# Attention and two expert layers on one core: where 1/sum is spread, how the V products are cut, and the order of two kinds of loads

## The chip, the cores and the metric

The kernel runs on one core of a Trainium2 chip. The metric is the device time of one launch in microseconds (us). The kernel before took 536.39 us, the median of three runs (535.16, 536.39, 536.76).

## What is computed

Attention over 2 batches and 8 heads (576 tokens, 64 dimensions a head) with rotated queries and keys; then two expert layers over the 1152 tokens, both in fp32:

```python
scores = scale * np.matmul(q_rot, k_rot.transpose(0, 1, 3, 2))
attn = np.exp(scores - np.max(scores, axis=-1, keepdims=True))
attn = attn / (np.sum(attn, axis=-1, keepdims=True) + 1e-09)
x = np.matmul(attn, v)                  # to (1152, 512)
h = np.maximum(x @ w_in, 0.0)           # w_in 512x2048
x = h * h @ w_out                       # w_out 2048x512
out = (x @ w_a) * (x @ w_b) @ w2_out    # w_a, w_b 512x1536, w2_out 1536x512
```

## The kernel before

**Who sets the order.** Every piece of work is an operation of a planner (`Plan`, lines 75 to 250). It names the engine or engines that may do it (`FLEX` is VectorE or GpSimd), a cost, the operations that it follows, and the buffers that it takes (`acq`) and gives back (`rel`). TensorE's operations keep the order in which the program writes them; for the other engines the planner plays the program through with its costs and takes, on each engine, the ready operation that is due first. `soon` (with `anchor`) makes an operation due a fixed time after another one, `urgent` lets an engine wait a little for it, and `pl.far` lets work that is due much later stand back. The kernel's engines then run these orders strictly, each waiting at semaphores.

**Attention.** The 16 heads go in 8 pairs (0 to 7). A pair has five score steps (`scores`, line 394): steps 0 to 3 are four TensorE matmuls for 128 queries of both heads (L415), step 4 is a shorter tail (L411). The scores land in one of two wide PSUM slots (`STAGS`, two because `NS` is 2). VectorE copies them out negated with the row minimum (L443, one for each head), ScalarE takes the exponential and the row sum (L448), VectorE transposes 32x32 blocks (L465). The main loop (lines 1080 to 1097) writes, for each step, the scores of the next step, the loads, the V products of the pair before, and the transpose.

**V products.** `times_v` (L501) multiplies 18 blocks of 32 keys, eight small matmuls each, into four PSUM banks (`AV`, columns 0 to 191 of each, accumulated over all 18 blocks). `PARTS` cuts the blocks into five parts, 4, 4, 4, 3 and 3; part c of pair p-1 stands behind the scores that follow step c of pair p. After the last part ScalarE copies the banks out (`xf`, eight copies, L318). The last pair's parts stand between the first pieces of expert layer 1 (`VFILL` says behind which).

**1/sum.** `recip` (L529) makes 1/sum and cuts it in three bf16 pieces. `flip` (L546) transposes these into rows; `spread` (L556) multiplies the rows by a selector, nine small matmuls (L564), so that 1/sum stands in 128 partitions over all queries; ScalarE copies that out in two halves (`inv`, L568); GpSimd multiplies it with `xf` (L587) and splits the result into high and low parts. In step 4 of pair p stand the flip of pair p-1 and the spread of pair p-2, both in one slot of `STAGS` (named r).

**Loads.** In each of steps 0 to 3 `load_part` issues one quarter of the pair's V (L481) and one plane of the keys and queries of pair p+2 (L341). One tiny ScalarE copy into the V buffer's first column (L479), behind the step's last exponential, releases both: SyncE's transfers then wait for that copy. GpSimd rotates the keys and queries (L367).

**Expert layers.** Products in fp32 are three matmuls of high and low halves (L719 to L721). Sixteen and twelve tiles of hidden columns are handled, most of them by a seven-product scheme (`product`, `super1`, `super2`). `split_y` (L839) makes the seven combinations of layer 1's result for layer 2: VectorE or GpSimd subtract (L610, tiles gT), ScalarE casts the high half (L613), VectorE or GpSimd subtract again for the low half. In `super2` the first products are moved out of PSUM by ScalarE (`p1`, `p7`, `p6`: L920, L925, L930) and added or multiplied by VectorE (`p2` L935, `p4` L940, `p5` L946); `p4` needs the bank that L925 empties, `p3` the one that L946 empties.

## Time and profile before

| | |
|---|---|
| median of three runs | 536.39 us |
| profiled execution | 535.2 us, of which the span of the trace is 533.4 us |
| granted TensorE clock | 0.999 of full speed |
| TensorE matmuls busy | 524.1 us (98%) |
| TensorE weight loads busy | 473.1 us (89%), beside the matmuls |
| VectorE busy | 421.1 us (79%) |
| ScalarE busy | 305.1 us (57%) |
| GpSimd busy | 397.4 us (74%) |
| attention, steady part | about 22 to 118 us |

Shares are means over stages with different limits. A timeline row gives the start of an instruction (or of several merged ones, with their count), its length, its engine and line, what it writes and reads, and in brackets the idle time before it with what ended it. Matmul lengths overlap by some 0.1 us, so the spacing of two starts, not the length, is what a piece of TensorE work takes.

### The profile page before, as it was taken

The page shows a single profiled execution, that of the slowest core. Times are in us where ns is not written, and L with a number is a line of the kernel's source. Part 1 is how long each engine was busy: PE and PEld are TensorE (multiplying, and loading weights), DVE is VectorE, ACT ScalarE, POOL GpSimd, SP SyncE. Part 2 cuts the span into 40 slices and gives each one's busy share as a digit, 9 for nine tenths or more (in the row PEclk, how much of TensorE's full clock was granted, in tenths as well). Part 3 has the DMA queues.
Part 4 walks back from the last instruction along what each step waited for, and adds up shares of the span by engine and source line. Part 5 has one row for each costly group of instructions (what it writes and reads, how often), then busy time and mean ns, then how long its engine had stood idle before and what let it go on. Part 6 is the DMA issues. An engine that isn't in the chain of part 4 may idle for free.

```text
span 533.4 us, 13367 instructions
## 1 busy us (share of the span) xinstructions
PE 524.1 (98%) x5390; PEld 473.1 (89%) x5390; DVE 421.1 (79%) x768; ACT 305.1 (57%) x756; POOL 397.4 (74%) x338
## 2 busy tenths in 40 slices
PE   8999999999999999999999998999999999999997
PEld 6666666668999999999999998999999999999996
DVE  5999997996996798678868999767878777878454
ACT  1767886897776784287348544766534444353210
POOL 2866889876998966776868799998888987776110
PEclk9999999999999999999999999999999999999999
...
GB/s 232 212 186 181 181 181 181 149 152 123 119 63 96 120 119 80 119 79 65 106 108 119 53 29 78 80 120 119 80 120 118 80 80 119 119 41 0 1 1 177
DMA packets 18913, 58.48 MB, mean 110 GB/s; under 512 B 2313, under 2 KB 4489, under 8 KB 17828
## 3 DMA queue, kind: packets, MB, share of 16 engines
...
q14 instruction: 19, 0.16, 0.1%
...
## 4 chain that ended last, share of the span: by engine, by line
PE 91%; POOL 3%; DVE 2%; issue 1%; DMA 1%; ACT 0%; SPq 0%; DVEq 0%
PE m L719 13%; PE m L721 13%; PE m L720 13%; PE av L501 9%; PE s L415 8%; PE av L721 6%; PE av L719 6%; PE av L720 6%; PE m L1037 3%; PE m L1038 3%; PE m L1039 3%; PE s L411 2%; PE av L1037 1%; PE av L1038 1%; PE av L1039 1%
## 5 line engine op out<-in xcount | busy, mean ns | idle before, releaser
L610 POOL TENSOR_TENSOR g<-v,g 128x576 fp32r<-128x576 f32 (+1 forms) x26 | 32.0, 1230 | 34.1 <-ACT g L736 34.1
L448 ACT ACTIVATE PV<-PV,st 128x576 f32<-128x576 f32 x48 | 36.9, 769 | 21.7 <-DVE PV L443 20.8
L367 POOL TENSOR_TENSOR X<-X,cs_rot 128x1152 f32<-128x1152 f32 x14 | 36.9, 2636 | 15.2 <-DMA X<-in_qk 13.9
L443 DVE TENSOR_SCALAR_CACHE_REDUCE PV<-s 128x576 f32<-128x576 f32 x48 | 34.5, 746 | 8.9 <-PE s L415 8.8
L772 DVE TENSOR_TENSOR oacc<-m,oacc 128x512 f32<-128x512 f32 (+1 forms) x31 | 21.0, 679 | 14.7 <-PE m L1039 14.6
L721 PE MATMUL m<-g,w_o 128*128 128x384 f32 (+1 forms) x99 | 31.9, 323 | 0.0
L720 PE MATMUL m<-g,w_o 128*128 128x384 f32 (+1 forms) x99 | 31.9, 322 | 0.0
L719 PE MATMUL m<-g,w_o 128*128 128x384 f32 (+1 forms) x99 | 31.9, 322 | 0.0
L920 ACT COPY v<-m 128x288 f32<-128x288 f32 x20 | 8.0, 398 | 39.2 <-PE m L721 39.2
L635 POOL TENSOR_SCALAR cl_i<-cl_i 128x512 f32<-128x512 f32 x14 | 27.2, 1949 | 2.1 <-ACT cl_i L626 2.1
L736 ACT CAST g<-v 128x576 fp32r<-128x576 f32 (+1 forms) x36 | 21.4, 595 | 10.5 <-DVE v L950 9.9
L720 PE MATMUL m<-x,w_pp 128*128 128x288 f32 x92 | 27.2, 295 | 0.0
L721 PE MATMUL m<-x,w_pp 128*128 128x288 f32 x92 | 27.2, 295 | 0.0
L719 PE MATMUL m<-x,w_pp 128*128 128x288 f32 x92 | 27.1, 294 | 0.0
L501 PE MATMUL av<-PT_wb,PV 32*64 32x160 f32 (+1 forms) x1152 | 25.5, 294 | 1.2 <-issue 1.2
L501 PEld LDWEIGHTS av<-PT_wb,PV 32*64 32x64 f32 x1152 | 19.6, 130 | 7.5 <-issue 6.1
L415 PE MATMUL s<-cs_rot 64*128 64x288 f32 x128 | 24.6, 434 | 1.6 <-DVE cs_rot L379 0.8
L415 PE MATMUL s<-rot 64*128 64x288 f32 x128 | 24.8, 433 | 0.7 <-DVE bits_i L632 0.7
L719 PE MATMUL m<-x,w_b 128*128 128x288 f32 x82 | 24.3, 296 | 0.9 <-DVE v L946 0.9
L501 PE MATMUL av<-PT_acc,PV 32*64 32x160 f32 (+1 forms) x1152 | 25.2, 294 | 0.0
L501 PEld LDWEIGHTS av<-PT_acc,PV 32*64 32x64 f32 x1152 | 19.8, 130 | 5.4 <-issue 4.1
L1037 PE MATMUL m<-w_b,g 128*128 128x512 f32 (+1 forms) x63 | 24.6, 390 | 0.0
...
## 6 DMA issues: line engine op xcount, KB each, us to landing
...
```

What stands on the lines that cost most here:

```text
L367: m = pl.op(where, ("s", 2 * S), lambda e, qi=qi: e.tensor_tensor(out=x()[:, :, qi, :], in0=x()[:, :, qi, :], in1=cs, op=ALU.mult), [done[ ...
L415: pe.matmul(s[h]()[:, bk, 0:288], q0, k0[h][:, bk * 288:bk * 288 + 288], start=True, stop=True)
L443: m = pl.op("DVE", ("us", 0.7), lambda e, h=h, j=j: e.tensor_scalar(out=PP[pr.k][:, h, :].rearrange("p (b n) -> p b n", b=2), in0=s[h]()[: ...
L448: x = pl.op("ACT", ("us", 0.8), lambda e, h=h, j=j: e.activation(PP[pr.k][:, h, :], PP[pr.k][:, h, :], AF.Exp, bias=st()[:, 0, j:j + 1], s ...
L501: pe.matmul(AV[a]()[half(h), q], v[r, h, b], pt[r, k:k + 4 + both, 32 * b:32 * b + 32], start=(b == 0), stop=(b == KB - 1), skip_group_che ...
L610: e.tensor_tensor(out=out_, in0=a, in1=b, op=ALU.subtract)
L635: e.tensor_scalar(out=dst(), in0=cl(), scalar1=-HI * TURN, scalar2=HI, op0=ALU.max, op1=ALU.min)
L719: pe.matmul(dst, wh, mh, start=first, stop=False, skip_group_check=open_)
L720: pe.matmul(dst, wh, ml, start=False, stop=False, skip_group_check=open_)
L721: pe.matmul(dst, wl, mh, start=False, stop=last, skip_group_check=open_)
L736: h = pl.op("ACT", ("p" if banked else "s", width), lambda e: e.copy(g()[:, 0, c], v()[:, 0:width]), after + first, acq=acq)
L1037: pe.matmul(b(), gt[:, 0, c], w[:, 0, d], start=(k == 0), stop=False)
```

## The change

Four things. (1) The spread of pair p-2 leaves step 4 of pair p and stands behind the scores of step 1 of pair p; it writes columns 192 to 479 of the first two banks of the V products, of which the products use columns 0 to 191, and the slot r now holds the flip alone. (2) The V products' parts are 2, 4, 4, 5 and 3 blocks. Of the last pair, 10, 5 and 3 blocks instead of 8, 4 and 6 stand behind the first pieces of layer 1. (3) Planes of keys and queries go ahead of the V quarters: two planes after step 0, one V quarter and a plane after step 1, two quarters after step 2, a quarter and a plane after step 3; each transfer has a ScalarE copy of its own that releases it, eight a pair instead of four (four in the last two pairs, which have no keys to load). (4) The y split of the second half is marked `pl.far`.

```diff
--- before.py
+++ after.py
@@ -31,21 +31,21 @@
 NPR = 5
 NS = 2
 KB = 18
-PARTS = ((0, 4), (4, 8), (8, 12), (12, 15), (15, 18))
+PARTS = ((0, 2), (2, 6), (6, 10), (10, 15), (15, 18))
+RUNS = tuple(k for k, (lo, hi) in enumerate(PARTS) if hi > lo)
 NG = 5
 NV = 3
 HB = 288
 PIECES = {"k0": (0, 288), "q0": (0, 192), "k1": (288, 576), "q1": (192, 320), "q2": (320, 576)}
 FIRST = (("k0", "cs"), ("k0", 1), ("q0", 0), ("k1", "cs"), ("k1", 1), ("q1", 0), ("q2", 0))
-VAT = ((0,), (1,), (2,), (3,), ())
-XAT = VAT
+LOADS = ((('x', 0), ('x', 1)), (('v', 0), ('x', 2)), (('v', 1), ('v', 2)), (('v', 3), ('x', 3)), ())
 FAR = 1.5
 WARM = (16, 2, 5, 3)
 EARLY, MID = 1, 4
 GATES = ((0,4),(6,1),(6,3))
 PACE = (27, 5)
 FILL = (-1,1,2,3)
-VFILL = (0,0,1,2,2)
+VFILL = (0,0,0,1,2)
 SOON = 6.0
 LATE = 3.0
 HASTE = 10.0
@@ -302,7 +302,7 @@
     MTAGS = tuple(BANKS)
     WTAGS = ("wa",) + tuple(f"wb{k}" for k in range(NWB))
     pl = Plan({
-        "raw": 3, "bits": 2, "sums": 1, "cl": 2, "wa": NWA, **{f"P{k}": 1 for k in range(NPR)}, **{f"v{k}": 1 for k in range(NV)}, "u": 2, "inv": 1,
+        "raw": 3, "bits": 2, "sums": 1, "cl": 2, "wa": NWA, **{f"P{k}": 1 for k in range(NPR)}, **{f"v{k}": 1 for k in range(NV)}, "u": 2, "inv": 1, "side": 1,
         **{t: 1 for t in STAGS + ("av",)}, **{t: 0 for t in TTAGS + MTAGS + WTAGS[1:]},
         "g0": 1, "g1": 1, "g2": 0, "g3": 0, "g4": 0,
     }, 6.0)
@@ -338,7 +338,7 @@
         if p:
             if p > 1:
                 for k, (qi, n) in enumerate(PLANES):
-                    LX[p, k] = lambda after, k=k, qi=qi, n=n: dma(288, lambda e: e.dma_start(out=b()[:, n, qi], in_=qk[p][:, n, qi]), after, acq=[] if k else [b])
+                    LX[p, k] = lambda after, k=k, qi=qi, n=n: dma(288, lambda e: e.dma_start(out=b()[:, n, qi], in_=qk[p][:, n, qi]), after)
                 return {}
             d = [dma(576, lambda e, qi=qi: e.dma_start(out=b()[:, :, qi], in_=qk[p][:, :, qi]), acq=[b] if qi else []) for qi in (1, 0)]
             return {(qi, n): d[1 - qi] for qi in range(2) for n in range(2)}
@@ -398,6 +398,9 @@
             ST[p] = lazy(lambda: st_p.tile([P, 2, 9], F32, tag="st", name=f"st{p}"))
         r = ROPE[p]
         tail = c == 4
+        side = []
+        if p > 1 and c == 1:
+            side.append(Buf("side", None))
         s = [Buf(STAGS, {t: (lambda t=t, h=h: sps.tile([P, 2, 512], F32, tag=t, name=f"s{p}_{c}_{h}")) for t in STAGS}) for h in range(1 if tail else 2)]
         pr = Buf(f"P{len(EXP) % NPR}", None)
         pr.k = len(EXP) % NPR
@@ -450,12 +453,11 @@
                 bias=st()[:, 0, j:j + 1], scale=-1.0, accum_out=st()[:, 1, j:j + 1]), [m])
             ex.append(x)
         EXP[p, c] = (pr, ex)
-        if tail and p:
+        if p > 1 and c == 1:
+            pl.op(None, None, None, spread(p - 2, side, [lambda h=h: AV[h]()[:, 192:480].rearrange("p (b n) -> p b n", b=2) for h in range(2)]), rel=side)
+        if p and tail:
             x = Buf(STAGS, {t: (lambda t=t: sps.tile([P, 2, 512], F32, tag=t, name=f"r{p}")) for t in STAGS})
-            ends = [flip(p - 1, [x], lambda: x()[:, 1].bitcast(BF16)[0:27, 896:1024])]
-            if p > 1:
-                ends += spread(p - 2, [], [lambda h=h: x()[:, h, 0:288].rearrange("p (b n) -> p b n", b=2) for h in range(2)])
-            pl.op(None, None, None, ends, rel=[x])
+            pl.op(None, None, None, [flip(p - 1, [x], lambda: x()[:, 1].bitcast(BF16)[0:27, 896:1024])], rel=[x])
 
     LV, zeros, fixed = {}, [], []
 
@@ -473,20 +475,28 @@
         more = p + 2 < NPAIR
         if c == 0 and more:
             load_qk_done[p + 2] = load_qk(p + 2)
-        w = ex[-1]
-        for a in VAT[c]:
-            r = slice(32 * a, 32 * a + 32)
-            w = pl.op("ACT", ("us", 0.2), lambda e, r=r: e.copy(V4[r, p % 2, 0, 0, 0:1], st()[r, 1, 2 * c + 1:2 * c + 2]), ex[-1:] + ([AVD[p - 2]] if p > 1 else []))
-            w.soon, w.anchor = 1.8, SDONE[p, c]
-            d = dma(288, lambda e, r=r: e.dma_start(out=V4[r, p % 2], in_=vq[p]), [w])
+        for i, (what, k) in enumerate(LOADS[c]):
+            i = min(i, len(ex) - 1)
+            j = 2 * c + i
+            if what == "x":
+                if not more:
+                    continue
+                qi, n = PLANES[k]
+                x = XA[p + 2]
+                w = pl.op("ACT", ("us", 0.2), lambda e, qi=qi, n=n, j=j: e.copy(x()[0:32, n, qi, 0:1], st()[0:32, 1, j:j + 1]), ex[i:i + 1], acq=[] if k else [x])
+                d = load_qk_done[p + 2][PLANES[k]] = LX[p + 2, k]([w])
+            else:
+                r = slice(32 * k, 32 * k + 32)
+                w = pl.op("ACT", ("us", 0.2), lambda e, r=r, j=j: e.copy(V4[r, p % 2, 0, 0, 0:1], st()[r, 1, j:j + 1]), ex[i:i + 1] + ([AVD[p - 2]] if p > 1 else []))
+                d = dma(288, lambda e, r=r: e.dma_start(out=V4[r, p % 2], in_=vq[p]), [w])
+                LV.setdefault(p, []).append(d)
+            w.soon, w.anchor = 1.0 + 0.7 * i, SDONE[p, c]
             d.late = FAR
-            LV.setdefault(p, []).append(d)
-        for k in XAT[c] if more else ():
-            d = load_qk_done[p + 2][PLANES[k]] = LX[p + 2, k]([w])
-            d.late = FAR
 
     def times_v(p, part):
-        if part == 0:
+        if part not in RUNS:
+            return
+        if part == RUNS[0]:
             AVB[p] = Buf("av", None)
         pt, v = PT[p % 2], V4[:, p % 2]
 
@@ -501,8 +511,8 @@
                         pe.matmul(AV[a]()[half(h), q], v[r, h, b], pt[r, k:k + 4 + both, 32 * b:32 * b + 32], start=(b == 0), stop=(b == KB - 1), skip_group_check=True)
 
         n = PARTS[part][1] - PARTS[part][0]
-        o = pl.op("PE", ("us", 0.05 + 0.255 * n), mm, TOK[p] + LV[p], acq=[] if part else [AVB[p]])
-        if part < len(PARTS) - 1:
+        o = pl.op("PE", ("us", 0.05 + 0.255 * n), mm, TOK[p] + LV[p], acq=[AVB[p]] if part == RUNS[0] else [])
+        if part < RUNS[-1]:
             return
         AVD[p] = o
         xf = XF[p] = vtile(f"xf{p}")
@@ -837,6 +847,11 @@
         pl.op(None, None, None, [t1, t2, t3, t4] + [o for i in range(3, 7) for o in XPART[t][i]], rel=[x])
 
     def split_y(t, b):
+        pl.far = t == 1
+        parts_y(t, b)
+        pl.far = False
+
+    def parts_y(t, b):
         if b == 0:
             YPART[t] = {}
 
```

**TensorE, the tail of a pair and the start of the next.** Before, L411 is the tail's scores, L549 the flip, L564 the spread into slot r, L501 the V products (av are their banks):

```order
L411 MATMUL s_4_0_1367<-rot 64x288 x4
L549 LDWEIGHTS part_1221
L549 MATMUL r_1376<-small,part_1221 27x128
...
L564 MATMUL r_1376<-rows_1135,small 128x128
...
L564 MATMUL r_1376<-rows_1135,small 128x64
L501 MATMUL av_242<-PT_wb,PV 64x160
```

After, L418 is the scores of step 1, L574 the spread, now into the banks av_248 and av_251, L511 the V products of the pair before:

```order
L418 MATMUL s_1_0_1491<-cs_rot 128x288
L418 MATMUL s_1_1_1496<-cs_rot 128x288
...
L574 MATMUL av_248<-rows_1446,small 128x128
...
L574 MATMUL av_251<-rows_1446,small 128x96
...
L574 MATMUL av_251<-rows_1446,small 128x64
L511 MATMUL av_248<-PT_acc,PV 64x160
```

The nine matmuls of the spread moved from the end of one pair to behind step 1 of the next, in front of the first V part there.

**ScalarE, from a pair's second step to its third.** Before, L448 is the exponential, L479 the release of a V quarter and a plane:

```order
L448 ACTIVATE PV,st_1178<-PV,st_1178 128x576
L479 COPY PV<-st_1178 32x1
L448 ACTIVATE PV,st_1178<-PV,st_1178 128x576 x2
L479 COPY PV<-st_1178 32x1
L448 ACTIVATE PV,st_1178<-PV,st_1178 128x576 x2
L479 COPY PV<-st_1178 32x1
L613 CAST x<-x_0_725 128x288
L448 ACTIVATE small,st_1178<-small,st_1178 128x576 x2
```

After, L451 is the exponential, L486 the release of a plane of keys and queries (X), L490 that of a V quarter, L578 the copy of 1/sum out of the V products' bank:

```order
L451 ACTIVATE PV,st_1204<-PV,st_1204 128x576
L486 COPY X_1286<-st_1204 32x1 x2
L451 ACTIVATE PV,st_1204<-PV,st_1204 128x576 x2
L578 COPY inv_1333<-av_248 128x288
L490 COPY PV<-st_1204 32x1
L578 COPY inv_1333<-av_251 128x288
L486 COPY X_1286<-st_1204 32x1
L451 ACTIVATE PV,st_1204<-PV,st_1204 128x576 x2
L490 COPY PV<-st_1204 32x1 x2
```

The two copies of 1/sum stand here now, between the exponentials of steps 1 and 2, with four releases around them where two stood.

**ScalarE at the y split.** Before, L920, L925 and L930 move products of layer 2 out of PSUM, and L613 casts pieces of the split (yacc is layer 1's result):

```order
L613 CAST x<-yacc 128x2x288
L920 COPY v_0_0_4396<-m_1988 128x288
L613 CAST x<-yacc 128x2x288
L925 COPY v_0_0_4396<-m_1977 128x288
L930 COPY u_0_4415<-m_1988 128x288
L613 CAST x<-gT_4387 128x2x288
```

After, L935, L940 and L945 are the moves, L623 the casts, L636 a step of a weight's conversion:

```order
L623 CAST x<-yacc 128x2x288
L636 ACTIVATE cl_4407<-raw_4270 128x512
L935 COPY v_0_0_4416<-av_251 128x288
L940 COPY v_0_0_4416<-av_248 128x288
L623 CAST x<-yacc 128x2x288
L945 COPY u_0_4440<-av_251 128x288
```

The second move out of PSUM now stands in front of the second pair of casts of yacc, not behind it.

**VectorE at the y split.** Before, L610 subtracts pieces of the split (gT), L935, L946 and L940 add from PSUM, L629 is a step of a weight's conversion:

```order
L629 TENSOR_SCALAR av_92<-cl_b_4323 128x512
L610 TENSOR_TENSOR gT_4387<-yacc,gT_4387 128x576
L935 TENSOR_TENSOR v_0_0_4396<-av_242,v_0_0_4396 128x288
L610 TENSOR_TENSOR gT_4387<-yacc,gT_4387 128x576
L946 TENSOR_TENSOR v_0_0_4396<-m_1988,v_0_0_4396 128x288
L940 TENSOR_TENSOR u_0_4415<-m_1977,u_0_4415 128x288
```

After, L620 subtracts, L950, L955 and L961 add from PSUM, L706 adds two pieces of a weight:

```order
L620 TENSOR_TENSOR gT_4405<-yacc,gT_4405 128x576
L950 TENSOR_TENSOR v_0_0_4416<-m_2015,v_0_0_4416 128x288
L706 TENSOR_TENSOR sums_p_4428<-sums_p_4428 128x256
L955 TENSOR_TENSOR u_0_4440<-av_248,u_0_4440 128x288
L961 TENSOR_TENSOR v_0_0_4416<-av_251,v_0_0_4416 128x288
L620 TENSOR_TENSOR parts<-gT_4405,parts 128x576
```

One of the two subtractions of gT in front of the last add from PSUM is gone from VectorE (GpSimd has it), and the add of weight pieces and the third product's add stand there.

## Rows read from the trace of the kernel before

**Rows 1.** Busy time by stage (windows view); first column the stretch in us, then each engine.

```profile
22.00:118.00 96.00, 94.10 (x2278) 64.17 (x2284) 87.47 (x175) 75.33 (x240) 74.69 (x76) 1.00 0.70 178
...
133.00:318.00 185.00, 185.00 (x1237) 184.09 (x1224) 150.98 (x280) 116.91 (x271) 148.22 (x117) 1.00 0.28 92
```

**Rows 2.** TensorE timeline of one pair (start, length, line, operation); a trailing bracket is idle time.

```profile
48.89 1.24 PE L415 MATMUL s<-rot 64*128 64x288 f32 x8
...
51.09 1.97 PE L415 MATMUL s<-rot 64*128 64x288 f32 x8
52.99 1.42 PE L501 MATMUL av<-PT_wb,PV 32*64 32x160 f32 x64
54.34 1.24 PE L415 MATMUL s<-rot 64*128 64x288 f32 x8
55.51 1.37 PE L501 MATMUL av<-PT_wb,PV 32*64 32x160 f32 x64
56.80 1.54 PE L415 MATMUL s<-rot 64*128 64x288 f32 x8
...
60.85 0.49 PE L564 MATMUL r<-rows,small 27*128 27x128 bf16 x9
61.27 1.09 PE L501 MATMUL av<-PT_wb,PV 32*64 32x160 f32 x48
62.29 1.25 PE L415 MATMUL s<-cs_rot 64*128 64x288 f32 x8
```

**Rows 3.** TensorE timeline, V products of pair 5; the bracket is idle time and its releaser.

```profile
90.52 0.49 PE L501 MATMUL av<-PT_wb,PV 32*64 32x128 f32 x4 [1.23 <-issue]
```

**Rows 4.** Waits between 22 and 118 us: total, times, longest.

```profile
POOL X L367 <- DMA X<-in_qk: 13.9, 6, 4.9
```

**Rows 5.** ScalarE timeline of the same pair.

```profile
55.68 0.19 ACT L479 COPY PV<-st 32x1 f32<-32x1 f32 x1
...
56.41 0.78 ACT L448 ACTIVATE PV<-PV,st 128x576 f32<-128x576 f32 x1
...
57.18 0.76 ACT L448 ACTIVATE PV<-PV,st 128x576 f32<-128x576 f32 x1
...
61.41 0.40 ACT L568 COPY inv<-r 128x288 f32<-128x288 f32 x1
```

**Rows 6.** VectorE timeline of the same pair.

```profile
55.61 0.76 DVE L443 TENSOR_SCALAR_CACHE_REDUCE PV<-s 128x576 f32<-128x576 f32 x1 [0.25 <-PE s L415]
...
59.59 1.38 DVE L465 STREAM_TRANSPOSE PT_acc<-PV 128x1152 f32<-128x1152 f32 x1
```

**Rows 7.** TensorE timeline near 324 and 328 us, where the y split stands.

```profile
323.92 0.40 PE L719 MATMUL m<-parts,w_b 128*128 128x288 f32 x1 [0.76 <-ACT v L925]
...
328.30 0.40 PE L719 MATMUL m<-x,w_b 128*128 128x288 f32 x1 [0.95 <-DVE v L946]
```

**Rows 8.** ScalarE timeline there.

```profile
322.89 0.67 ACT L613 CAST x<-yacc 128x576 fp32r<-128x576 f32 x1 [1.64 <-DVE yacc L772]
323.47 0.39 ACT L925 COPY v<-m 128x288 f32<-128x288 f32 x1
```

**Rows 9.** VectorE timeline there, and the same operation earlier.

```profile
304.57 0.76 DVE L610 TENSOR_TENSOR gT<-yacc 128x576 f32<-128x576 f32 x1
...
324.00 1.97 DVE L610 TENSOR_TENSOR gT<-yacc,gT 128x576 f32<-128x576 f32 x1 [0.54 <-POOL gT L610]
...
326.26 1.62 DVE L610 TENSOR_TENSOR gT<-yacc,gT 128x576 f32<-128x576 f32 x1
327.81 0.44 DVE L946 TENSOR_TENSOR v<-m,v 128x288 f32<-128x288 f32 x1
```

**Rows 10.** GpSimd timeline there.

```profile
322.56 2.79 POOL L610 TENSOR_TENSOR gT<-yacc 128x576 f32<-128x576 f32 x2
...
327.23 5.24 POOL L610 TENSOR_TENSOR parts<-gT,parts 128x576 fp32r<-128x576 f32 x3
```

## Prediction, written before the changed kernel ran

> **What bounds the kernel now.** I read the stages first. Between 22 and 118 us, the steady attention, matmuls are busy 94.1 of 96.0 us, and VectorE 87.5 [rows 1]; between 133 and 318 us they are busy in all of 185.0 us [rows 1]. So TensorE's own work sets the time nearly everywhere, and a change that gives it the same work can only move its stalls. The number of its instructions is the same after, apart from where they stand. There are four kinds of stall to look at.
>
> First, inside a pair of heads. The TensorE timeline of pair 3 [rows 2] runs from 48.89 to 62.29, a period of 13.40 us; I count from its start, S0 = 48.89. An undisturbed score step is 1.24 long, as at 54.34 and 48.89. Step 1 is 1.97 (0.73 too long) and step 3 is 1.54 (0.30 too long) [rows 2]: the step's second head waits there for a PSUM slot, that is, for VectorE's copy out. That is 1.03 us a pair, and no bracket shows it, since merged rows hide it. Second, one bare stall of 1.23 us in the V products of pair 5, with "issue" as its releaser, so nothing that the program waits for [rows 3]. Third, two stalls of TensorE at the y split, 0.76 us behind a ScalarE move and 0.95 us behind a VectorE add [rows 7]. Fourth, GpSimd waits 13.9 us in all for keys and queries [rows 4]; GpSimd rotates them a pair ahead, no row of TensorE waits for that, and so I count nothing for it.
>
> **The steady pairs.** Prices on TensorE, by the spacing of starts in [rows 2]: a part of 4 blocks takes 56.80 - 55.51 = 1.29, a part of 3 blocks 62.29 - 61.27 = 1.02; so 0.27 a block on top of 0.21. A part of 2 blocks is then 0.75 and one of 5 blocks 1.56. The spread takes 61.27 - 60.85 = 0.42.
>
> Behind step 1 there stood 4 blocks, 54.34 - 52.99 = 1.35 (with a short wait for ScalarE's copies of xf). Now spread and 2 blocks stand there: 0.42 + 0.75 = 1.17, so step 2 starts 0.18 earlier. Its scores were waited for by VectorE, which stood idle 0.25 in front of their copy [rows 6], so VectorE follows by those 0.18, and the 0.30 of step 3 stays as it is, only earlier. Behind the tail there stood spread and 3 blocks, 1.44; now 5 blocks, 1.56: 0.12 more. The 0.73 of step 1 lies between VectorE's copies of steps 0 and 1, with 3 blocks between the two steps before and after; it stays. Sum for a pair: -0.18 + 0.12 = -0.06; for pairs 2 to 6, -0.3.
>
> Pair 1 has no spread. Its V parts behind steps 1 to 4 go from 4, 4, 4 and 3 blocks to 2, 4, 4 and 5. Less stands where VectorE's copy of step 1 holds step 2 anyway, and more stands where TensorE runs free: two blocks, 0.54, come back in the last part, and of the two that leave I credit only 0.18, what VectorE's idle time gave in the pair above. That is +0.36; the bounds are 0 (all of it gained) and +0.54 (none). In pair 7 the 10, 5 and 3 blocks between layer 1's first pieces are the same 18; in pair 6 eight blocks run at the end where six and a spread ran, 2 x 0.27 - 0.42 = +0.12, against which the 0.18 behind step 1 may stand if VectorE has room there. Attention in all: -0.3 + 0.36 + 0.12 = +0.2 us, between -0.5 and +0.7.
>
> **What the moved spread makes ScalarE and TensorE wait for.** The copies of 1/sum used to read the slot r; now they read two banks into which V products run. TensorE's part in front of them must have ended, and the next part must wait for them. By the order of the changed program they wait for the part behind step 2, which ends about 0.1 to 0.2 before 56.80, S0 + 7.7. ScalarE ended step 1's exponentials before the release at 55.68, S0 + 6.8 [rows 5]. So it now stands idle nearly a microsecond, then does two copies of 1/sum at 0.40 [rows 5] that overlap by 0.1 and a release or two of 0.19, and is free at about S0 + 8.6. The exponentials of step 2, which began at 56.41 = S0 + 7.5 and ended at 57.94 = S0 + 9.05 [rows 5], now run from 8.6 to 10.2. What waits for them is VectorE's transpose at 59.59 = S0 + 10.7 [rows 6], after the shift S0 + 10.5. Some 0.3 us is left: hidden, and I cost it at nothing. The next part of the V products that must wait for the copies stands behind step 3, which begins at 56.80 and takes 1.54 less 0.1 of overlap, so at S0 + 9.2 after the shift, and has 0.6 left. If that cover is gone, VectorE's transposes and copies come late one after the other, step 3 and the tail with them, and each pair pays. Four more releases a pair (eight for four) are 4 x 0.19 = 0.8 us of ScalarE at most, which sat idle 0.2 of its time in this stage [75.3 of 96.0, rows 1]. Bounds for the whole edit: 0 and, at 0.8 a pair in five pairs, +4.
>
> [...] Were the copies free to run beside the products, the microsecond of idle ScalarE would be gone, and the sum would be the same as long as it is hidden.
>
> **Loads.** A plane of keys and queries is a step earlier on average, a V quarter a step later for some of them. The last V quarter is still released after step 3's exponentials, as before, so the V products of that pair wait for nothing later than now. The gain is in GpSimd's 13.9 us, off the path: 0.
>
> **The y split.** The 0.76 us stall [rows 7]: TensorE waited for the move L925, at 323.47; ScalarE was behind a cast at 322.89, which itself had waited 1.64 us for an add of VectorE [rows 8]. In the changed order the move stands in front of that cast. The stall goes, -0.76; bounds 0 (if another instruction is late in its place) and -0.76. The 0.95 us stall: VectorE's last add L946 at 327.81 stood behind a subtraction of 1.62 us and, before, one of 1.97 [rows 9]. The same operation took 0.76 at 304.57 [rows 9]: it is stretched beside GpSimd, which worked on the same split from 322.56 to 325.35 and again from 327.23 on [rows 10]. In the changed order one subtraction is gone from VectorE, and a 256-wide add and another product's add of about 0.44 come in its place; I estimate these at 0.8 to 1.3 instead of 1.62, so the stall is 0.3 to 0.8 shorter; I take 0.45. Bounds: -0.95 (all of it) and, if VectorE's remaining subtraction is held up by the one that GpSimd now does, +0.5. Sum -1.2, between -1.7 and +0.5.
>
> [...]
>
> The planner also deals out the rest of the two expert layers anew, on three engines. Before there is no stall at all in 185 us [rows 1], so this can only lose; with nothing against it in the changed order I take 0, with +1.5 as the other end.
>
> **Sum.** +0.2 for attention, 0 for the waits, 0 for loads, -1.2 for the y split: -1.0 us. The profiled execution took 535.2 us (its span of 533.4 and 1.8 around it), 1.2 less than the median of 536.39; against it the sum gives 534.2, and against the median 535.4 us.
>
> **Rivals.**
> A. ScalarE becomes the bound of a pair (slower). Place: the copies of 1/sum between the exponentials of steps 1 and 2. It decides once ScalarE is over 0.3 us later than I reckon, at VectorE's transpose of step 2. For it: one wait moves ScalarE's step 2 by 1.1 us, and the margin is my own arithmetic on rows of 0.1 us. Against it: ScalarE catches up in step 3, where it has idle time. Price 0.4 to 0.8 in each of five pairs, +2 to +4, mean 3; with the other terms 536.4 - 1.0 + 3.0 = 538.4 us. Chance 0.16.
> B. More goes than I credit: both y stalls entirely (-1.7) and the bare issue stall of pair 5 (-1.2), which stands at a place where the program has changed. With +0.2: -2.7, 533.7 us. For it: nothing in the program waits at 90.52. Against: the same stall can come at another place. Chance 0.24.
> C. The change only shuffles: the stalls of the y split come again at a neighbouring instruction, as the same casts and subtractions must still be done in time by GpSimd and VectorE: +0.2, 536.6 us. Chance 0.20.
> My forecast has the rest, 0.40; its own range is 534.4 to 536.2.
>
> **Numbers.** About 0.3%, 1.6 us, is what a measurement can tell from none: below 534.8 is faster, above 538.0 slower. Faster: B's 0.24 and a third of the forecast's 0.40, as its own range reaches below 534.8: 0.38. Slower: most of A, and 0.03 for a new stall in the layers: 0.16. Same: 0.46. The range goes from 533.2, which is B with attention at its better bound (-0.5 for +0.2 is 0.7 less, of which I take most), to 538.0, just short of A's mean.
>
> **What would show it.** In the TensorE timeline after: about 13.35 us a pair; spread and two blocks together 1.2 behind step 1; step 1 still near 1.97 and step 3 near 1.54. In ScalarE's: an idle bracket of nearly 1 us in front of L578 with TensorE's V products as releaser. At the y split: no wait for the move L940, and a shorter one for L961. I am wrong if step 3 or the tail shows a wait for VectorE above 0.4, if V products wait for L578, or if matmuls between 133 and 318 us are no longer busy throughout.

## The result and the profile after

The changed kernel takes 538.86 us (median of six runs, 537.91 to 540.15), the kernel before 536.01 us beside it (six runs, 534.53 to 536.82): a ratio of 1.0064, 95% interval 1.004 to 1.0088. It is 2.85 us slower, where 1 us faster was forecast. The profiled execution took 537.91 us, its span is 535.8 us (533.4 before).

By stage (windows view, columns as in [rows 1]; the number behind the engines is the granted TensorE clock):

```profile
22.00:118.00 96.00, 92.37 (x2195) 62.78 (x2195) 84.62 (x169) 75.17 (x257) 74.81 (x78) 0.98 0.66 173
...
133.00:318.00 185.00, 185.00 (x1269) 183.84 (x1268) 149.46 (x275) 118.13 (x277) 147.62 (x120) 1.00 0.29 94
```

The layers' long stretch is again without a gap, 185.0 of 185.0. The loss is in attention: 92.37 us busy of 96 where it was 94.10 [rows 1], at a mean clock of 0.98. Layer 1 begins (first matmul with w_i) at 122.88 us, before at 120.12: 2.75 us lost by then. Behind that point 0.37 us come back, so that the spans differ by 2.4.

An undisturbed pair does what was worked out. This is pair 2 (TensorE timeline, columns as in [rows 2]; the first row is the start of the same pair in the kernel before, the others are of the changed kernel):

```profile
35.52 1.24 PE L415 MATMUL s<-cs_rot 64*128 64x288 f32 x8
...
35.65 1.24 PE L418 MATMUL s<-cs_rot 64*128 64x288 f32 x8
...
39.66 0.49 PE L574 MATMUL av<-rows,small 27*128 27x128 bf16 x9
40.08 0.80 PE L511 MATMUL av<-PT_acc,PV 32*64 32x160 f32 x32
40.81 1.24 PE L418 MATMUL s<-cs_rot 64*128 64x288 f32 x8
...
47.31 1.64 PE L511 MATMUL av<-PT_acc,PV 32*64 32x160 f32 x80
48.88 1.24 PE L418 MATMUL s<-rot 64*128 64x288 f32 x8
```

The spread takes 0.42, the part of 2 blocks 0.73 (40.08 to 40.81), that of 5 blocks 1.57 (47.31 to 48.88), and the pair 13.23, where it took 13.37 before (35.52 to 48.89). But the next pairs took 13.97, 13.89, 14.54 and 13.66 us from start to start (before 13.40, 13.55, 15.11 with its stall, 13.39), and from the start of pair 7 to layer 1 went 17.93 us, where 15.79 stood before: of the 2.75 us, 2.14 are lost there. The TensorE timeline shows where:

```profile
60.01 1.19 PE L414 MATMUL s<-rot 64*64 64x288 f32 x8 [0.45 <-DVE small L446]
...
65.50 0.62 PE L511 MATMUL av<-PT_wb,PV 32*64 32x160 f32 x17 [0.69 <-issue]
66.05 1.24 PE L418 MATMUL s<-cs_rot 64*128 64x288 f32 x8
...
91.07 0.29 PE L511 MATMUL av<-PT_wb,PV 32*64 32x160 f32 x1 [0.67 <-issue]
...
107.52 0.52 PE L511 MATMUL av<-PT_acc,PV 32*64 32x128 f32 x13 [0.38 <-issue]
...
112.36 1.40 PE L418 MATMUL s<-rot 64*128 64x288 f32 x6 [1.31 <-DVE bits_i L642]
113.68 2.44 PE L511 MATMUL av<-PT_wb,PV 32*64 32x160 f32 x64
```

The kernel before had one stall with "issue" as its releaser [rows 3]; here there are three in this view, and two more by the starts of single instructions (in the tail's scores at 102.58, and at 60.01, where VectorE, named in the bracket, had ended its copy at 59.59). A stall is not wholly lost time: the step at 66.05 takes 1.24 behind the stall at 65.50, where step 1 of pair 3 takes 1.97 with its wait for a slot. The last two rows are another matter: TensorE waits 1.31 us for the conversion of the first weight, which uses a score slot, and then 4 blocks of V products take 2.37 us (113.68 to 116.05) instead of 1.30. The windows of that time show why (last columns: granted clock, DMA share, GB/s):

```profile
111.00:112.00 1.00, 0.04 (x1) 0.00 (x0) 0.97 (x2) 0.98 (x5) 0.00 (x0) 1.00 0.00 0
...
113.00:114.00 1.00, 1.00 (x16) 0.42 (x21) 1.00 (x2) 1.00 (x3) 0.90 (x2) 0.62 0.75 172
114.00:115.00 1.00, 1.00 (x44) 1.00 (x34) 1.00 (x5) 0.97 (x4) 1.00 (x2) 0.50 1.08 402
...
116.00:117.00 1.00, 1.00 (x10) 0.77 (x8) 0.12 (x1) 0.88 (x3) 0.83 (x1) 0.67 0.17 47
```

TensorE was busy 0.04 of the microsecond from 111 on; from 113.24 on the granted clock is 0.50 of full speed, for 3.41 us (the trace's clock records). Nothing of the kind is in attention before, where it is 1.00 throughout [rows 1], though the same wait is there, with 0.66 us (TensorE timeline before, then VectorE's after):

```profile
111.17 1.21 PE L415 MATMUL s<-rot 64*128 64x288 f32 x6 [0.66 <-DVE bits_i L632]
```

```profile
109.24 0.76 DVE L446 TENSOR_SCALAR_CACHE_REDUCE PV<-s 128x576 f32<-128x576 f32 x1 [0.73 <-PE s L418]
```

VectorE does the conversion behind its copies of step 1's scores, and these come late, as VectorE waits 0.73 us for the scores: the stall at 107.52 stands in front of step 1.

ScalarE and VectorE in pair 3, S0 = 48.88 (they answer to [rows 5, 6]):

```profile
56.78 0.40 ACT L578 COPY inv<-av 128x288 f32<-128x288 f32 x1 [1.14 <-PE av L511]
...
57.55 0.77 ACT L451 ACTIVATE PV<-PV,st 128x576 f32<-128x576 f32 x1
...
58.32 0.76 ACT L451 ACTIVATE PV<-PV,st 128x576 f32<-128x576 f32 x1
```

```profile
59.52 1.37 DVE L467 STREAM_TRANSPOSE PT_acc<-PV 128x1152 f32<-128x1152 f32 x1
```

ScalarE does stand idle 1.14 us for the V products before it copies 1/sum, and the exponentials of step 2 end at S0 + 10.2; the transpose that needs them starts at S0 + 10.6 behind VectorE's own copy, without a bracket. The cover held.

At the y split (TensorE timeline, answering to [rows 7]):

```profile
324.58 0.40 PE L729 MATMUL av<-parts,w_b 128*128 128x288 f32 x1 [0.27 <-ACT v L935]
...
329.95 0.40 PE L729 MATMUL av<-x,w_b 128*128 128x288 f32 x1 [0.35 <-DVE v L961]
...
336.24 0.40 PE L729 MATMUL m<-x,w_pp 128*128 128x288 f32 x1 [0.47 <-DVE v L961]
```

The two stalls are 0.27 and 0.35 instead of 0.76 and 0.95, and a third of 0.47 is new behind them. From 318 to 345 us TensorE is idle 1.09 us (25.91 busy of 27.00), before 1.71.

### The profile page after: what moved, and what is told of

Its sections match the earlier page's. It is cut to its first block, busy times and chain, and to the rows that moved or that the text cites. A ratio compares the mean times of both kernels' runs of the same rounds, so it can differ in the third digit from the quotient of the medians.

```text
span 535.8 us, 13402 instructions
## 1 busy us (share of the span) xinstructions
PE 524.2 (98%) x5390; PEld 472.2 (88%) x5390; DVE 424.2 (79%) x764; ACT 306.2 (57%) x780; POOL 398.6 (74%) x342
## 4 chain that ended last, share of the span: by engine, by line
PE 91%; DVE 6%; DMA 1%; issue 1%; SPq 0%; DVEq 0%
PE m L729 13%; PE m L731 13%; PE m L730 13%; PE av L511 9%; PE s L418 8%; PE av L731 6%; PE av L730 6%; PE av L729 6%; PE m L1052 3%; PE m L1053 3%; PE m L1054 3%; PE s L414 2%; PE av L1052 2%; PE av L1053 2%; PE av L1054 2%; DMA X<-in_qk 1%
## 5 line engine op out<-in xcount | busy, mean ns | idle before, releaser
L620 POOL TENSOR_TENSOR g<-v,g 128x576 fp32r<-128x576 f32 (+1 forms) x24 | 29.4, 1225 | 32.0 <-ACT g L746 30.2
L451 ACT ACTIVATE PV<-PV,st 128x576 f32<-128x576 f32 x48 | 36.9, 768 | 20.8 <-DVE PV L446 20.6
L731 PE MATMUL m<-g,w_o 128*128 128x384 f32 (+1 forms) x105 | 33.7, 321 | 0.0
L730 PE MATMUL m<-g,w_o 128*128 128x384 f32 (+1 forms) x105 | 33.7, 321 | 0.0
L729 PE MATMUL m<-g,w_o 128*128 128x384 f32 (+1 forms) x105 | 33.6, 320 | 0.0
L511 PE MATMUL av<-PT_wb,PV 32*64 32x128 f32 (+1 forms) x1152 | 26.9, 303 | 1.4 <-issue 1.4
L418 PE MATMUL s<-cs_rot 64*128 64x288 f32 x128 | 24.0, 433 | 2.7 <-DVE cs_rot L379 2.0
L645 POOL TENSOR_SCALAR cl_i<-cl_i 128x512 f32<-128x512 f32 x13 | 25.3, 1952 | 1.4 <-ACT cl_i L636 1.0
L418 PE MATMUL s<-rot 64*128 64x288 f32 x128 | 24.9, 438 | 1.3 <-DVE bits_i L642 1.3
L511 PEld LDWEIGHTS av<-PT_wb,PV 32*64 32x64 f32 x1152 | 20.4, 135 | 6.4 <-issue 4.8
L511 PE MATMUL av<-PT_acc,PV 32*64 32x160 f32 (+1 forms) x1152 | 25.3, 294 | 0.4 <-issue 0.4
L731 PE MATMUL m<-x,w_b 128*128 128x288 f32 x82 | 24.2, 295 | 0.0
L730 PE MATMUL m<-x,w_b 128*128 128x288 f32 x82 | 24.2, 295 | 0.0
L511 PEld LDWEIGHTS av<-PT_acc,PV 32*64 32x64 f32 x1152 | 19.5, 130 | 5.3 <-issue 4.1
L729 PE MATMUL m<-x,w_b 128*128 128x288 f32 x82 | 24.1, 294 | 0.0
L620 POOL TENSOR_TENSOR w_pp<-sums_p,w_pp 128x512 fp32r<-128x512 f32 (+1 forms) x16 | 19.8, 1253 | 5.6 <-ACT w_pp L623 5.6
L645 POOL TENSOR_SCALAR cl_o<-cl_o 128x512 f32<-128x512 f32 x11 | 21.4, 1956 | 1.4 <-ACT cl_o L636 1.4
L418 PEld LDWEIGHTS s<-cs_rot 64*128 64x128 f32 x128 | 13.5, 185 | 10.0 <-DVE PV L446 3.5
```

Of the source, the lines that this page charges most:

```text
L418: pe.matmul(s[h]()[:, bk, 0:288], q0, k0[h][:, bk * 288:bk * 288 + 288], start=True, stop=True)
L451: x = pl.op("ACT", ("us", 0.8), lambda e, h=h, j=j: e.activation(PP[pr.k][:, h, :], PP[pr.k][:, h, :], AF.Exp, bias=st()[:, 0, j:j + 1], s ...
L511: pe.matmul(AV[a]()[half(h), q], v[r, h, b], pt[r, k:k + 4 + both, 32 * b:32 * b + 32], start=(b == 0), stop=(b == KB - 1), skip_group_che ...
L620: e.tensor_tensor(out=out_, in0=a, in1=b, op=ALU.subtract)
L645: e.tensor_scalar(out=dst(), in0=cl(), scalar1=-HI * TURN, scalar2=HI, op0=ALU.max, op1=ALU.min)
L729: pe.matmul(dst, wh, mh, start=first, stop=False, skip_group_check=open_)
```

## What the issue stalls are

The page's line of the DMA queue for instructions has 42 packets of 0.69 MB. The trace has 10,780 matmuls and weight loads on TensorE and 46 instructions that wait at semaphores or drain, 10,826 in all. That is 16 KB, about 258 of these instructions, a packet.

```profile
PE 524.2 (98%) x5390; PEld 472.2 (88%) x5390; DVE 424.2 (79%) x764; ACT 306.2 (57%) x780; POOL 398.6 (74%) x342
...
q8 instruction: 42, 0.69, 0.5%
```

I numbered all of TensorE's instructions in the order of their starts, in both traces: matmuls and weight loads, and those that wait at semaphores or drain, since without these the remainder drifts. Every issue stall stands at the same remainder by 256, which is 193: at instructions 1985, 2241, 3521, 4033 and 4289 after the change, at 3521 before. There are 42 boundaries with that remainder and 42 packets, one to each. I read the packet that starts next after such a boundary has been passed in attention as the one with the instructions behind the following boundary: TensorE ran on past the first before it started, and in the six stalls went on behind the second 2.26 to 2.86 us after it had. Times in us, from the transfer records and the instructions' starts (not a view of the profile):

```
                 boundary   packet   next boundary   TensorE     packet start
                 passed     starts   reached         goes on     to going on
before, pair 5    84.42      87.66     89.00           90.52        2.86
after,  pair 3    48.51      52.91     55.48           55.48        (no stall)
after,  pair 3    55.48      57.75     59.49           60.01        2.26
after,  pair 4    59.49      62.70     64.52           65.50        2.80
after,  pair 5    86.54      88.50     90.10           91.07        2.57
after,  pair 6    97.97     100.03    102.06          102.58        2.55
after,  pair 7   102.06     105.03    106.84          107.52        2.49
```

So in the stalls a packet was used 2.3 to 2.9 us after it started, and it started late: after the change between 0.4 and 4.4 us behind the boundary in attention, while the loads of keys, queries and V ran. In the layers most packets start ahead of their boundary, by 0.2 to 3.4 us. TensorE stalled where it ran through 256 instructions sooner than that: in both traces at the six boundaries that it reached 1.3 to 2.0 us after the packet's start, and at none that it reached 2.2 us or more after it.

V products are dense in instructions. In the trace each of the program's matmuls in the scores and V products is two matmuls and two weight loads (a part of 4 blocks, 32 of the program's, stands there as x64); so a block is 32 instructions in 0.27 us, a score step 16 in 1.17. Five blocks, a step and three blocks are 272 instructions in 3.77 us (47.31 to 51.08). In an undisturbed pair, stretches of 256 instructions that take less than 4.0 us are 8% of all before and 15% after; less than 3.6 us, 2% and 10% (counted from the starts, pairs 3 and 4 before, pair 2 after). The five blocks before the next pair's first step and the three behind it made that.

## The experiments

The theories: F, instructions come late behind the loads, and the phase (where in the program the boundaries fall) decides where it hurts; D, on top of F, V blocks that stand close together make it worse; L, the new order of loads makes it; A, ScalarE's copies of 1/sum (my rival A); C, the clock. "Gaps" below are the spacings above 0.35 us between two TensorE instructions at a boundary of 256, summed from 24 us to the start of layer 1, in the one profile of each run.

| run | V parts | gaps, us | layer 1 begins | median, us | ratio to before (95%) |
|---|---|---|---|---|---|
| before | 4,4,4,3,3 | 1.5 | 120.1 | 536.0 | |
| e2, loads only | 4,4,4,3,3 | 0 | 118.6 | 535.2 | 0.9993 (0.9972 to 1.0014) |
| e12, the same again | 4,4,4,3,3 | 1.4 | 119.1 | 535.1 | 0.9983 (0.9959 to 1.0008) |
| e8, loads and mark | 4,4,4,3,3 | 0.5 | 118.8 | 534.8 | 1.0009 (0.9977 to 1.0042) |
| e7, old parts | 4,4,4,3,3 | 0 | 121.3 | 543.5 | 1.015 (1.0106 to 1.0194) |
| e11, spread only | 4,4,4,3,3 | 0 | 132.0 | 546.9 | 1.0195 (1.0157 to 1.0233) |
| e9, even parts | 3,4,4,4,3 | 0 | 118.7 | 541.2 | 1.0098 (1.0063 to 1.0133) |
| e16, even, no mark | 3,4,4,4,3 | 0 | 119.7 | 539.1 | 1.0077 (1.0054 to 1.0099) |
| e13, even, other fill | 3,4,4,4,3 | 2.1 | 120.1 | 540.4 | 1.0104 (1.0064 to 1.0144) |
| e15, four and four | 2,4,4,4,4 | 2.6 | 119.4 | 542.5 | 1.0137 (1.0106 to 1.0169) |
| after | 2,4,4,5,3 | 3.7 | 122.9 | 538.9 | 1.0064 (1.004 to 1.0088) |
| e5, after again | 2,4,4,5,3 | 3.8 | 124.3 | 539.9 | 1.011 (1.0066 to 1.0154) |
| e1, old loads | 2,4,4,5,3 | 3.6 | 122.4 | 537.7 | 1.0033 (1.0009 to 1.0056) |
| e3, phase | 2,4,4,5,3 | 2.9 | 124.0 | 539.2 | 1.0062 (1.0037 to 1.0086) |
| e6, clock kept busy | 2,4,4,5,3 | 5.6 | 122.4 | 541.2 | 1.0122 (1.0096 to 1.0147) |
| e10, no mark | 2,4,4,5,3 | 4.2 | 122.9 | 539.5 | 1.0058 (1.0031 to 1.0085) |
| e14, other fill | 2,4,4,5,3 | 4.1 | 121.6 | 542.5 | 1.015 (1.0123 to 1.0176) |
| e4, half the loads | 2,4,4,5,3 | 1.0 | 119.2 | 537.0 | 1.002 (0.9997 to 1.0043) |

**e1: the old loads in the changed kernel.**

```diff
-LOADS = ((('x', 0), ('x', 1)), (('v', 0), ('x', 2)), (('v', 1), ('v', 2)), (('v', 3), ('x', 3)), ())
+VAT = ((0,), (1,), (2,), (3,), ())
+XAT = VAT
```

> The changed kernel with the loads and releases of the kernel before (one V quarter and one plane a step, one release copy); spread, parts and the y split as changed. The changed kernel's trace stalls TensorE at "issue" in pairs 3 to 7 where the one before stalls once; each of these stalls stands at a whole multiple of 256 TensorE instructions, some 2.5 us behind the start of a 16 KB instruction transfer that came late. Theory F (instruction transfers come late behind the loads, and the phase decides where it hurts): the issue stalls move, and their sum may be less or more; the pairs without one stay at 13.2 to 13.3 us; pair 7's wait for the early weight's conversion stays; 536 to 539.5 us. Theory L (the new order of the loads is what makes them late): the issue stalls go back to one, at most 537.3 us. Theory A (ScalarE's copies of 1/sum hold up the pairs): nothing changes, 538.5 to 539.2 us.

3.6 us of gaps, as in the changed kernel; L falls. The pairs without one stay at 13.40, and the clock did not fall in attention in this profile (1.00 over the whole span), which fits its 1.2 us less (by the medians, 537.7 for 538.9). A falls with the undisturbed pairs of the changed kernel.

**e2 and e12: the new loads alone in the kernel before.**

```diff
-VAT = ((0,), (1,), (2,), (3,), ())
-XAT = VAT
+LOADS = ((('x', 0), ('x', 1)), (('v', 0), ('x', 2)), (('v', 1), ('v', 2)), (('v', 3), ('x', 3)), ())
```

> The kernel before with the new loads and their eight releases only. Theory F: the clean pairs stay at 13.4 us, the issue stalls come at other places than at 89 us and sum up to anything between 0 and 3 us: 535 to 538 us. Theory L: two or more issue stalls more than before, 537 to 538.5 us. Theory A (the copies of 1/sum are the cause): as before, 535.5 to 536.5 us.

> The kernel before with the new loads alone, timed in five rounds: the best so far by its profile (attention ends at 118.6 us, no issue stall). If this holds, 0.5 to 1 us faster than the kernel before, 534.5 us; if the one issue stall of the kernel before is there in some executions only, no difference.

Pairs of 13.4 us where nothing disturbs them, gaps of 0 and 1.4 us in two profiles of the same program: the lengths vary from execution to execution. The new loads do no harm; that they help can't be told from no change.

**e3: another phase.** The warming matmuls of pair 0 are halved in width and doubled in number.

```diff
-            for k in range(n):
-                pe.matmul(b()[:, 0:P], ZERO, ZERO, start=True, stop=True)
+            for k in range(n if n == WARM[0] else 2 * n):
+                w = P if n == WARM[0] else P // 2
+                pe.matmul(b()[:, 0:w], ZERO, ZERO[:, 0:w], start=True, stop=True)
```

> The changed kernel, with each warming matmul of pair 0 (but the first 16) cut in two of half the width: the same columns in twice the instructions, 88 TensorE instructions more before the first V product and nothing else. Theory F: every boundary of 256 instructions comes 88 instructions (about 1.8 us) earlier in the program, so the issue stalls at 60.0, 65.5, 91.1, 102.6 and 107.5 us go or move to other instructions, again at whole multiples of 256 from each other, and the time changes by up to 2 us either way, without any change in the work of the pairs. Theories L and A: the stalls stay where they are in the program, and the time within 0.3 us of the changed kernel's.

The gaps left the five places and came at 106.38 (1.58) and 123.18 (1.35), at instructions 4289 and 5057, which with 88 instructions more in front are other places of the program, and boundaries again. That speaks for F; pairs 4 and 5, without one, took 13.44 and 13.32. The time says little, as pair 1 began 1.9 us later, the narrow matmuls being slower than reckoned.

**e4: half the loads.**

```diff
-                d = dma(288, lambda e, r=r: e.dma_start(out=V4[r, p % 2], in_=vq[p]), [w])
+                d = dma(288, lambda e, r=r: e.dma_start(out=V4[r, p % 2], in_=vq[p]), [w]) if p < 3 else w
```

> The changed kernel without the V loads of pairs 3 to 7 (their release copies stay, the products read the V of an earlier pair): half of the loads' bytes from pair 3 on. Theory F: instruction transfers start within 1.5 us of the boundary that asks for them, no issue stall above 0.3 us from pair 4 on, and pairs 4 to 6 take 13.2 to 13.4 us each: 2 to 2.5 us less than the changed kernel, about 536.5 us. Theory A: pairs 3 to 6 keep their 13.6 to 14.5 us, since ScalarE does the same work: 538.5 us or more.

From pair 3 on the V quarters are not loaded, so that the output is not attention's. Pairs 3 to 6 took 13.32 us each, to the hundredth, and from pair 3 to layer 1 every boundary was passed without a gap above 0.35; in pairs 1 and 2, with full loads, there are two (starts of pairs 3 to 7, TensorE timeline):

```profile
49.95 1.24 PE L418 MATMUL s<-rot 64*128 64x288 f32 x8
...
63.28 1.24 PE L418 MATMUL s<-cs_rot 64*128 64x288 f32 x8
...
76.60 1.24 PE L418 MATMUL s<-rot 64*128 64x288 f32 x8
...
89.92 1.24 PE L418 MATMUL s<-cs_rot 64*128 64x288 f32 x8
...
103.24 1.24 PE L418 MATMUL s<-rot 64*128 64x288 f32 x8
```

The instruction packets of the ten boundaries in pairs 3 to 6 start 0.89 us behind them on average, where it is 2.25 after the change and 1.69 before. The same work of ScalarE, VectorE and TensorE with fewer transfers has no stall, and its packets come sooner: this shows F, with one profile. It also prices an undisturbed changed pair at 13.32, 0.08 less than before. From the start of pair 3 to layer 1 it takes 69.2 us, the changed kernel 74.0 and the kernel before 71.2, of which 1.5 are its one stall. Little of that shows in the median, since what follows takes 2.3 us more than in the changed kernel: a gap of 2.25 stands among the last pair's products.

**e5: the changed kernel again.**

> The changed kernel once more, unaltered, with a new profile. Theory F: the boundaries of 256 TensorE instructions are at the same places of the program, so the issue stalls come at the same ones (5 of them between 59 and 108 us before), with lengths that differ by some tenths, since the loads land differently each time; 538 to 540 us. If the stalls came at other places altogether, theory F would lack its reason. The halving of the granted clock at 113 us may be there or not: theory C (the clock explains the loss) expects a run without it to be 1.2 us faster.

Three of the five places are the same (instructions 3521, 4033, 4289), two went and one came (1473). The clock halved again, at 114.9 us (0.997 over the span, as after the change). Theory F fits, with chance in it.

**e6: TensorE kept busy in pair 7's wait**, by four matmuls into unused columns.

```diff
+                if (p, c) == (NPAIR - 1, 2):
+                    for k in range(4):
+                        pe.matmul(s[0]()[:, 0, 384:512], rot[half(0), 0, c * P:(c + 1) * P], rot[half(0), 1, 0:P], start=True, stop=True)
```

> The changed kernel with four extra matmuls (128 columns, into unused columns of the score bank) in pair 7 between the first and second head of step 2, where TensorE stands idle 1.3 us and the granted clock then falls to half for 3.4 us. They shift every later boundary of 256 instructions by 16. Theory C: the clock does not fall there, and the time is 1.2 us less, 537.5 us. Theory F: no more than 0.5 us, as pair 7's length is set by the early weight's conversion and the late instructions: 538.3 us or more.

The clock stayed at 1.00, the 4 blocks took 1.30 again, and from pair 7's start to layer 1 went 17.03 instead of 17.93 us. But boundary gaps of 5.6 us, and one of 2.1 us among the last pair's products, took more than that: that the clock sets the time isn't shown, only that it costs time at that place.

**e7: the old parts in the changed kernel.**

```diff
-PARTS = ((0, 2), (2, 6), (6, 10), (10, 15), (15, 18))
+PARTS = ((0, 4), (4, 8), (8, 12), (12, 15), (15, 18))
-VFILL = (0,0,0,1,2)
+VFILL = (0,0,1,2,2)
```

> The changed kernel with V products in 4, 4, 4, 3 and 3 blocks as before (and 8, 4 and 6 for the last pair); the moved spread, the loads and the y split stay. Behind step 1 stand spread and 4 blocks, 1.7 us instead of 1.2. Theory D (5 blocks before and 3 behind the next pair's first step make TensorE ask for 256 instructions within 3.4 us too often): fewer issue stalls, 536.5 to 537.5 us, although each pair's work is about 0.1 us longer. Theory F without D (phase alone): the stalls move, and their sum may be anything; 536 to 539.5 us. Theory A: the copies of 1/sum stay where they are, 538.5 us or more.

No gap at a boundary, as D has it, but pairs of 13.8 to 14.3 us: spread and 4 blocks behind step 1 bring step 2 late. And 7 us are lost in the layers, which are dealt anew: TensorE waits 2.0 us for VectorE near 190 us and 2.6 for ScalarE's move at the y split, and the clock halves twice (0.994 over the span).

**e8: the mark on the y split added to e2.**

```diff
     def split_y(t, b):
+        pl.far = t == 1
+        parts_y(t, b)
+        pl.far = False
```

> The kernel before with the new loads and the marked y split, without the moved spread and with the old parts. Attention as in the run of the loads alone (no issue stall): pairs of 13.4 us. At the y split, if the mark alone does what the changed kernel shows there, 0.6 us less: 534.6 us. If the y split's stalls are decided by the whole deal of the layers, anything between -0.5 and +1 us of the run of the loads alone: 534.7 to 536.2 us.

The y split's idle time (318 to 345 us) is 1.47 us, where 1.70 stood with the loads alone: the mark does not bring what the changed kernel gains.

**e9, e13 and e16: even parts**, with 11, 4 and 3 blocks of the last pair (`VFILL` as in the changed kernel), with 7, 4 and 7, and with these but without the mark.

```diff
-PARTS = ((0, 2), (2, 6), (6, 10), (10, 15), (15, 18))
+PARTS = ((0, 3), (3, 7), (7, 11), (11, 15), (15, 18))
```

> The changed kernel with parts of 3, 4, 4, 4 and 3 blocks: behind the tail stand 4 blocks instead of 5 (32 TensorE instructions fewer in a row there), behind step 1 spread and 3. The issue stalls of all runs so far: 3.8 to 7.7 us in the profiles of the five kernels with parts 2, 4, 4, 5, 3 and the full loads, 0 to 1.5 us in the four with 4, 4, 4, 3, 3. Theory D (the five blocks before the next pair's first step ask for instructions too fast): the stalls fall to 2 us or less, and attention ends (first matmul of layer 1) at 119.5 to 121 us instead of 122.9. Theory F without D (phase alone): 3 us of stalls or more are as likely as none.

> The changed kernel with parts of 3, 4, 4, 4 and 3 blocks, and of the last pair's 7, 4 and 7 behind the first pieces of layer 1 (10, 5 and 3 as changed; 8, 4 and 6 before). Theory D (many V blocks close together ask for instructions faster than they come): no boundary stall above 0.5 us in attention, as in the run with even parts, and none at the last pair's products either, where 11 and 10 blocks with little between them stalled 1.8 to 2.3 us in four profiles: the fourth piece of layer 1 begins at 131.5 to 133.5 us (133.1 before, 136.1 after). The layers behind, dealt anew, may lose 0 to 4 us: 534.5 to 539 us.

> The run with even parts and 7, 4 and 7 blocks of the last pair, without the mark on the y split: attention the same, and another deal of the layers behind it. If it is luck of the deal where the layers lose, 534 to 539 us, and the waits for VectorE near 188 us (3 us in the run with even parts) come or go with it.

One block fewer before the step: 0, 2.1 and 0 us of gaps, and attention ends 2.7 to 4.1 us sooner than after the change. In all nine profiles with the old or even parts the gaps are 0 to 2.1 us, in the seven with the changed parts and full loads 2.9 to 5.6. So D holds beyond the chance that e2 and e12 show, two profiles of one program with 0 and 1.4. In e9 the last pair's 11 blocks in a row stalled instead (TensorE timeline):

```profile
121.02 2.91 PE L511 MATMUL av<-PT_acc,PV 32*64 32x160 f32 x144
125.78 0.80 PE L511 MATMUL av<-PT_acc,PV 32*64 32x160 f32 x32 [1.84 <-issue]
```

With 7, 4 and 7 blocks this is gone (e13: 0.3, e16: none). None of the three is fast, as 4 to 7 us are lost behind attention (in e9 that stall is 2.1 of 7.3), at several places: in e13 TensorE waits for ScalarE's move at the y split (waits from 318 to 350 us; total, times, longest):

```profile
PE m L729 <- ACT u L945: 2.6, 1, 2.6
```

**e10: the changed kernel without the mark; e14: with 6, 4 and 8 blocks of the last pair.**

```diff
-        pl.far = t == 1
```

```diff
-VFILL = (0,0,0,1,2)
+VFILL = (0,0,1,2,2)
```

> The changed kernel without the mark on the y split. Attention as in the changed kernel (ends at 122.5 to 124.5 us). At the y split: if the mark brought the 0.6 us that the changed kernel gains there, the two stalls of the kernel before are back (0.8 and 0.9 us idle); if the reshuffled layers brought them, they stay at 0.3 and 0.4.

> The changed kernel with its parts of 2, 4, 4, 5 and 3, but of the last pair's 6, 4 and 8 blocks instead of 10, 5 and 3 behind the first pieces of layer 1. Theory D: the boundary stalls between 30 and 110 us stay (3 us or more in all), the one at 125 to 130 us goes. 537.5 to 541 us.

Gaps of 4.2 and 4.1 us, three of five places in each as in the changed kernel. Without the mark the y split is better still, 0.39 us idle:

```profile
318.00:345.00 27.00, 26.61 (x195) 25.73 (x195) 26.92 (x39) 13.83 (x29) 26.64 (x20) 1.00 0.19 60
```

So the deal of the layers brings that gain, not the mark. In e14 the gap among the last pair's products is gone as expected, and the layers lose 5.6 us.

**e11: the spread moved, nothing else.**

```diff
+        if p > 1 and c == 1:
+            pl.op(None, None, None, spread(p - 2, side, [lambda h=h: AV[h]()[:, 192:480].rearrange("p (b n) -> p b n", b=2) for h in range(2)]), rel=side)
-            if p > 1:
-                ends += spread(p - 2, [], [lambda h=h: x()[:, h, 0:288].rearrange("p (b n) -> p b n", b=2) for h in range(2)])
```

> The kernel before with the spread moved and nothing else. Behind step 1 stand spread and 4 blocks, 1.7 us where 1.35 stood; behind the tail 3 blocks without the spread. Pairs of 13.4 us if VectorE takes the shift up at the tail, as the sum of TensorE's work says; 13.8 us, as in the run with the old parts, if step 2 comes late for VectorE and this is not made good. Theory D: no issue stall above 0.5 us. With 13.8 us a pair, attention ends at 121.5 us and the time is 538 us.

I missed here: 16.8 us a pair, 3.4 more. In this program the planner set ScalarE's copies of 1/sum ahead of step 1's exponentials, not behind (timelines of ScalarE and TensorE):

```profile
57.16 0.70 ACT L570 COPY inv<-av 128x288 f32<-128x288 f32 x2 [1.23 <-PE av L503]
...
58.87 0.78 ACT L451 ACTIVATE PV<-PV,st 128x576 f32<-128x576 f32 x1
```

```profile
61.86 1.24 PE L418 MATMUL s<-rot 64*128 64x288 f32 x6 [1.54 <-DVE PV L446]
63.02 2.44 PE L503 MATMUL av<-PT_wb,PV 32*64 32x160 f32 x64
```

ScalarE waits 1.23 us for V products with two steps' exponentials behind it, step 3's second head waits 1.54, and the clock halves in four pairs (0.987 over the span): the 4 blocks at 63.02 take 2.37 instead of 1.30. So the wait and the clock share the 3.4 us. This is rival A's mechanism, further up in ScalarE's order than in the changed kernel.

**e15: four blocks before and four behind the step.**

```diff
-PARTS = ((0, 2), (2, 6), (6, 10), (10, 15), (15, 18))
+PARTS = ((0, 2), (2, 6), (6, 10), (10, 14), (14, 18))
```

> The changed kernel with parts of 2, 4, 4, 4 and 4: 4 blocks before and 4 behind the next pair's first step, so 8 around it as in the changed kernel (5 and 3), and 7 in the run with even parts. Theory D: what counts is the sum around that step, 256 instructions within some 3.4 us; stalls as in the changed kernel, 2.5 us or more in all, attention ends at 121.5 us or later. Theory D5 (five blocks in one part are what hurts): 1 us of stalls or less, attention ends at 119 to 120 us.

2.6 us of gaps, as D has it (8 blocks around the step, as after the change), but attention ends at 119.4, as D5 has it, since three of its pairs take 13.03 to 13.31. So e15, with one profile, does not tell the sum around the step from the five blocks in one part.

## Why the prediction was wrong

The sum held for what it summed. Step by step: spread, 2 and 5 blocks cost 0.42, 0.73 and 1.57 in pair 2 (0.42, 0.75 and 1.56 said; in pairs 3 and 5 the 2 blocks took 0.86 and 1.02); the pair gained 0.14 where it is undisturbed, 0.08 in e4 (0.06 said); steps 1 and 3 kept their waits in pair 3, 1.97 and 1.54; pair 1 lost 0.30 (0.36 said). ScalarE's idle time, its exponentials and the slack came as worked out, and rival A did not come. That its mechanism is real e11 shows, where it costs more than the 0.4 to 0.8 a pair that I gave it. The new loads cut GpSimd's wait for keys and queries from 13.9 to 3.1 us and gave nothing, as said.

The step that failed is the second kind of stall, "one bare stall", which "nothing that the program waits for" explains. I took it as fixed, and in rival B as something that could go or move, not grow. The runs show it as the delivery of TensorE's instructions (in e4, with fewer loads, their packets started 0.89 us behind the boundary instead of 2.25, and from pair 3 to layer 1 no gap was above 0.35), and a change that moves V products moves the demand for them. "The number of its instructions is the same" was true and beside the point: what counted is how many stand close together (gaps of 2.9 to 5.6 us with the changed parts and full loads, 0 to 2.1 with the old or even ones). The gaps in attention rose from 1.5 to 3.7 us. Not all of that is lost, since a stall can take the place of a wait that would have come anyway, as in pair 4: pairs 2 to 6 together are 0.48 us longer, with 1.5 us of gaps more. The bracket of 0.45 for VectorE in front of the tail at 60.01 looks like a sign that I named of being wrong, a wait for VectorE above 0.4; it is a boundary as well.

Pair 7 failed with it, and there most of the loss is: I counted 0.12 us and got 2.14. The gap at 107.52 is 0.67. The wait for the early weight's conversion was in the trace before as well, with 0.66 us, and I left it out; now it is 1.31. Two things made it: the parts behind step 1 are shorter, so that TensorE comes to the wait sooner, and the gap makes VectorE's conversion late. With 2 blocks behind step 1 the wait is 0.85 and 0.86 where no gap stands in front of it (e3, e4), and 1.31 or 1.32 in the four other profiles with a gap at the same boundary (e5, e10, e14, e15); with 3 blocks it is 0.27 and 0.28 without a gap (e9, e16) and 0.58 with one (e13). The halved clock costs about 1.2 (1.07 on 4 blocks, the rest on step 3). It fell there in two of the five profiles with 1.31, so it is not bound to the wait.

The y split was mis-sized: -0.62 for -1.2. The first stall lost 0.49 of the 0.76 that I took off: TensorE no longer waits for the move L940, but 0.27 for the move L935 stands in its place. The second lost 0.60 (0.45 said), and a third of 0.47 came behind them, which was rival C's mechanism in part. The rest of the layers, which I put at 0 with +1.5 as the other end, lost 0.25 in this kernel; by e7, e9, e13 and e14, where 4 to 7 us are lost behind attention, that was luck, and the end was too near.

What stays open: why a packet starts 4.4 us late at one boundary and 0.4 at another is only seen together with the loads, not followed through the queues; and why the clock halves after some idle stretches of TensorE and not after others (e6 had a gap of 2.1 us without it) isn't settled. The shares above are those of one profiled execution of each kernel; the spans of these differ by 2.4 us, the medians by 2.85. No version beat the kernel before beyond doubt.
